# First projection units by feature block in a two-attention gated kernel on one Trainium2 core

## The chip, the core and the metric

The kernel runs on one core of one Trainium2 chip. The profile shows five engines and their queues: PE (matrix products; its weight loads are the row PEld), DVE (VectorE), ACT (ScalarE), POOL (GpSimd) and SP (SyncE), which here issues every DMA transfer. SBUF is the working memory, PSUM holds what PE writes, DRAM holds inputs, outputs and scratch. The metric is the device time of one execution in microseconds, lower is better; the time before is 1057.04 us, the median of three runs (1056.77 to 1057.28).

## The reference, cut to what matters

```python
x = A_x                                            # 1 x 2048 x 448
g = sigmoid((x * gate_w).sum(-1, keepdims=True))
# A: per-head feature maps (two softmaxes of q @ w_phi and k @ w_phi), then linear attention, @ wo
# B: softmax attention over all 2048 keys, 16 heads of 28
q, k, v = split_heads(x @ B_wqkv)
p = softmax(q @ k.T * 28 ** -0.5)
b = (p @ v).merged_heads @ B_wo
return g * a + (1 - g) * b
```

Everything is float32. The part that the change touches is `x @ B_wqkv` for the 896 columns of q and k of attention B.

## The kernel before

**Products in two parts.** A float32 operand is split into a high part of type fp32r and the rest. `XH` holds the high part of x (features on the partitions, in four blocks b of 128; positions along the free axis), `XL` the rest; a weight tile holds the high part in `w[:, 0]` and the rest in `w[:, 1]`. A product is high·high + low·high + high·low. The fourth block has only 64 features of its own: its upper 64 partitions hold a copy, from which the high part is taken away (L340), so that it needs two products. `x3` (L110) yields these in order, so a sum over 448 features takes 11 products (4 blocks × 3, less one).

**Projection units.** `UNITS` (L527) lists pairs (m, t): 128 columns of q and k, 512 positions. `proj_qk(n, ev)` (L532) takes a PSUM bank, runs the 11 products, copies the high part out on ACT (L540), takes the rest on DVE (L541), and stores both to DRAM (`qkd`, L542), from where later stages load heads. Units 0 to 3 are (m = 0..3, t = 0), units 4 to 7 are t = 1, units 8 to 11 t = 2, units 12 to 15 t = 3; then the columns m = 4.

**The start.** The raw data go through a pool `stg` of 4 buffers of [128, 2, 512]; the results of units through `ev`, 3 buffers. `load_cols(m)` loads 128 columns of the weight for all four feature blocks, `x_loads(t)` loads 512 positions of x in two transfers of two blocks. `splits(n)` splits the weight columns of unit n (n < 4) and x for t = n / 4 when n is a multiple of 4; it is called one unit ahead. The copies of high parts are on ACT, the subtractions on DVE, that of block 2 of x on GpSimd for t > 0 (L338). So unit 0 needs all of x's four blocks for t = 0 and the first 128 weight columns, unit 1 the next 128 columns, and so on.

**The loop** (L589) runs units 0 to 19. At n = 0, 4, 8 it asks for the next 512 positions of x; at n = 5 for `phi_s` and the four pieces of `wtk` (`load_fold`); at n = 10 for the second weight tile `wB1` and for the head tiles `qp`, `kp`, `kt` of the maxima; at n = 10, 12, 14, 17 it calls `fold`, which multiplies w_phi into a weight (L356) in a bank of the tag "s"; from n = 16 on `mx_unit` computes row maxima of q·k in tiles of two banks (`ps_mx`, two buffers).

**Who sets the order.** On PE, DVE, ACT and GpSimd instructions stand in the order of the program. On SP a planner sets the order of the transfers when the program is built; SP then works through that order, and a transfer whose condition isn't met holds up those behind it. Each transfer also waits until the one eight places before it in the queue has landed.

**PSUM banks.** `ps_s` (L61) hands out 3 banks by turns, `ps_pv` one bank, `ps_mx` two tiles of two banks each. A bank or tile can be written again when its readers are done.

**Later.** After the loop come the features of attention A, the folding of `wqA` (L717 to L721, in halves for the first two groups), the values, and from about 360 us on the scores of attention B.

Of the kernel before, what the change touches and what calls it, by code (L numbers as in the profile page):

```python
# [34 lines left out]
def f32(ap):  # L35
    return ap.bitcast(F32)
# [3 lines left out]
def gated_mix_kernel(ctx, tc, xT, wqkB, wvB, wvA, wkAT, wqAT, phi, woA, woB,  # L40
# [20 lines left out]
    def ps_s(nm):  # L61
        return ps.tile([P, 512], F32, tag="s", name=nm, bufs=psn[0])
# [266 lines left out]
    def split_x(t, raws):  # L329
        tt = slice(t * 512, (t + 1) * 512)  # L330
        for b, raw in zip((0, 2), raws):
            nc.scalar.copy(XH[:, b:b + 2, tt], raw)  # L332

            def low(b=b, raw=raw):
                if b == 0:
                    nc.vector.tensor_sub(XL[:, 0:2, tt], raw, f32(XH[:, 0:2, tt]))
                else:
                    (nc.gpsimd if t else nc.vector).tensor_sub(  # L338
                        XL[:, 2, tt], raw[:, 0, :], f32(XH[:, 2, tt]))
                    nc.vector.tensor_sub(XH[64:, 3, tt], raw[64:, 1, :], f32(XH[64:, 3, tt]))  # L340

            lows.append(low)
# [2 lines left out]

    def load_fold(src, nm):
        wts[nm] = bk.tile([112, NG, 512], F32, tag="wt", name=f"wt{nm}", bufs=1)
        for k in range(NG):
            nc.sync.dma_start(wts[nm][:, k, :], src[:, k, :])

# [181 lines left out]
    def proj_qk(n, ev):  # L532

        m, t = UNITS[n]
        tt = slice(t * 512, (t + 1) * 512)
        pq = ps_s(f"pqk{t}_{m}")
        w, c = wB[m // 4], m % 4 * P
        run(pq, [(w[:, i, b, c:c + P], x) for b, x, i in x3(tt)])
        e = ev.tile([P, 2, 512], F32R, tag="ev", name=f"ev{t}_{m}")
        nc.scalar.copy(e[:, 0, :], pq)  # L540
        nc.vector.tensor_sub(e[:, 1, :], pq, f32(e[:, 0, :]))  # L541
        nc.sync.dma_start(qk_d[m * P:(m + 1) * P, :, tt], f32(e))  # L542


    ev_s = ExitStack()
    ev = ev_s.enter_context(tc.tile_pool(name="ev", bufs=3))
    stg = ev_s.enter_context(tc.tile_pool(name="stg", bufs=4))
    wB[0] = weights(1, "wB0")
    wB[1] = ev.tile([P, 2, 4, 384], F32R, name="wB1", bufs=1)
    wkA_s = weights(2, "wkA_s")  # L550
    wvA_s = weights(3, "wvA_s")
    raws = {}

    def load_cols(m):
        raw = stg.tile([P, 2, 512], F32, tag="stg", name=f"wB0_raw{m}")[:, 0, :]
        raws[("c", m)] = raw = raw.rearrange("p (b n) -> p b n", n=P)
        nc.sync.dma_start(raw, wqkB[:, :, m * P:(m + 1) * P])

    def split_cols(m):
        split_weight(wB[0], raws.pop(("c", m)), slice(0, 4), slice(m * P, (m + 1) * P))  # L560

    def loads(key, *fns):
        raws[key] = [f() for f in fns]
# [9 lines left out]

    def splits(n):

        if n < 4:
            split_cols(n)
        if n % 4 == 0 and n < 16:
            split_x(n // 4, raws.pop(("x", n // 4)))
        if n in (13, 15):  # L580
            split_part(wB[1], "wB1", 384, (n - 13) // 2)
        take_lows()

    load_cols(0)
    x_loads(0)
    for m in (1, 2, 3):
        load_cols(m)
    splits(0)
    for n in range(NP):  # L589
        take_acts()  # L590
        if n in (0, 4, 8):
            x_loads(n // 4 + 1)
        if n == 5:
            nc.sync.dma_start(phi_s, phi)
            load_fold(wkAT, "k")
        if n == 10:
            part_loads("wB1", wqkB[:, :, 512:896], 384, "wB1")
        splits(n + 1)
        if n == 14:
            part_loads("wvA", wvA, 450, "wvA")  # L600
            nc.sync.dma_start(sel_s, sel)
            nc.sync.dma_start(mask_s, mask)
            for v in vap:
                nc.gpsimd.memset(v[:, :, 28:32], 0.0)
                nc.gpsimd.memset(v[:, :, 28:29], 1.0)
        if 16 <= n < 20:
            mx_unit()
        proj_qk(n, ev)
        if n in (16, 18):
            split_part(wvA_s, "wvA", 450, (n - 16) // 2)  # L610
            take_lows()
        if n == 0:
            pkv = ps_pv("pkv")
        if n in (10, 12, 14, 17):
            fold(wkA_s, "k", {10: 0, 12: 1, 14: 2, 17: 3}[n])
        if n == 10:
            pair_query(0, 0)
            pair_load(0, 0)
        if n == 15:
            pair_load(0, 1)  # L620
            pair_query(0, 1)
        if n in (14, 19):
            take_subs()
# [27 lines left out]
    for i in range(2 * NT + 11):  # L651
        t, q = i, i - NT
        y = q - 1
        tb = y // 2
        take_acts()
        if t < NT and t % 2 == 0:
            mx_unit()
            passes = (55 if t < NT - 4 else 44) + (4 if t >= 4 else 0)
            pace["n"], pace["at"] = 4 if t >= 4 else 0, [k * passes // 4 for k in (1, 2, 3)]
        if q in (0, 1):  # L660
            take_exps()

        if t % 2 == 0 and 0 <= t - 4 < NT:
            kv_add(t - 4)
            kv_add(t - 3)
        if q == 2:
            bk_s.close()
            ta_s = ExitStack()
            ta = ta_s.enter_context(tc.tile_pool(name="ta", bufs=1, reuse_waits="tile"))
            stg = ta_s.enter_context(tc.tile_pool(name="stg", bufs=2, reuse_waits="tile"))  # L670
            KV = ta.tile([112, 8, 64], F32, name="KV")
            kvT = kv_copy()
            ps_s_.close()
            ps = ps_s_.enter_context(tc.tile_pool(name="psq", bufs=1, space=PSUM, reuse_waits="tile"))
            psn[0] = 4
            woA_s = weights(3, "woA_s")
            wvB_s = weights(2, "wvB_s")
            take_exps()
        if t < NT:
            pk = ps_s(f"pk{t}")  # L680
            tok_major(pk, t, wkA_s, D, tick)
            fk[t] = features1(pk, f"k{t}", nc.gpsimd)
            take_exps(1)
        if 0 <= q < NT:
            pq = ps_s(f"pq{q}")
            tok_major(pq, q, wqA_s, D)
        if q == 0:
            fk[NT - 1] = features2(fk[NT - 1], f"k{NT - 1}")
        if q in (1, 2):
            fq[q - 1] = features2(fq[q - 1], f"q{q - 1}")  # L690
        if 0 <= q < NT:
            fq[q] = features1(pq, f"q{q}", nc.vector if 0 < q < 9 else nc.gpsimd)
        if 0 <= t - 1 < NT - 1:
            fk[t - 1] = features2(fk[t - 1], f"k{t - 1}")
        if q in (0, 1) or q >= 8:
            mx_unit()
        if y >= 9 and y % 2 and tb - 4 < 8:
            oTs[tb - 4] = normalize4(ta, num.pop(tb - 4), f"a{tb - 4}", 2)
        if q > 0:
            take_exps(int(q < NT))  # L700
        if q == 3:
            kv_out(kvT)
        if 2 <= q - 1 < NT:
            fq[q - 1] = features2(fq[q - 1], f"q{q - 1}")
        take_subs()
        if t == 1:
            pair_load(0, 3)
        if y >= 8 and y % 2 == 0 and tb - 4 < 8:
            num[tb - 4] = normalize3(*num[tb - 4], 2)
        if t < NT:  # L710
            value_a(t)
            if t % 2 and t < NT - 4:
                proj_qk(NP + t // 2, ev)
        if q in (0, 1):
            proj_qk(NP + 6 + q, ev)
        take_lows()
        if 2 <= i < 4:  # L717
            fold(wqA_s, "q", i - 2, 0, 2)
            fold(wqA_s, "q", i - 2, 2, 2)
        elif 4 <= i < 6:  # L720
            fold(wqA_s, "q", i - 2)  # L721
        if q == 1:
            ev_s.close()
        if q == 2:
            part_loads("woA", woA, D, "woA")
        if q == 11:
            part_loads("wvB", wvB, D, "wvB")
        if q in (4, 6):
            split_part(woA_s, "woA", D, (q - 4) // 2)
        if q in (14, 17):  # L730
            split_part(wvB_s, "wvB", D, (q - 14) // 3)
        if q == 1:
            gates()
        if y >= 4 and y % 2 == 0 and tb - 2 < 8:
            numer(tb - 2)
        if y < 9 or y % 2:
            if y >= 2 and y - 2 < NT:
                turn(y - 2)
        if 0 <= y - 10 < NT:
            out_a(y - 10)  # L740
            out_a2(y - 10)
        if y >= 9 and y % 2 == 0 and y - 2 < NT:
            turn(y - 2)
        if NT + 3 <= q < NT + 10:
            mx_unit()
        if q == NT + 2:
            bd_s.close()
            vb = [value_tile(0)]
        if 0 <= q - NT - 2 < 8:
            value_b(q - NT - 2)  # L750
        if y >= 5 and y % 2 and tb - 2 < 8:
            num[tb - 2] = normalize2(ta, *num[tb - 2], f"a{tb - 2}", 2, True)
# [383 lines left out]
```

## Time and profile before

| | |
|---|---|
| median of three runs | 1057.04 us |
| the profiled execution's own time | 1057.58 us |
| its span in the profile | 1055.8 us |
| PE busy | 1043.1 us |
| DVE, ACT, POOL busy | 705.1, 726.8, 227.7 us |
| moved by DMA | 99.03 MB |

The span runs from the first to the last instruction; what lies around it is 1.78 us here. Times in the rows are from the span's start. A row of the timeline has the start, the length, the engine, the line, what is written from what, how many instructions were merged (x2, x4), and in brackets how long the engine had stood idle and what released it. PE's products overlap, so that a product's rate is read from start to start, not from its length. In a row of windows stand, for each engine, the busy time and the number of instructions, then the granted TensorE clock, the share of the time in which the DMA engines moved packets, and the rate.

### The profile page before, as it was taken

The numbers are of one execution on the slowest core, as the hardware profiler recorded it, in microseconds if no ns is written. First come the engines' busy times: TensorE is split into PE (matmuls) and PEld (weight loads), VectorE is DVE, ScalarE is ACT, GpSimd is POOL, SyncE is SP. The second block draws the span as 40 slices with busy tenths as digits, with TensorE's granted clock in tenths as the row PEclk, the third lists the DMA queues.
The fourth block names the chain that finished last, engine by engine and source line by source line (L and its number), as shares of the span: only waits on it lengthen the run. The fifth ranks groups of instructions, "written<-read, shape, count | busy, mean of one in ns | idle before, by whom it ended". The sixth has DMA issues, their size and how long they took to land.

```text
span 1055.8 us, 16548 instructions
## 1 busy us (share of the span) xinstructions
PE 1043.1 (99%) x6328; PEld 566.3 (54%) x6328; DVE 705.1 (67%) x871; ACT 726.8 (69%) x879; POOL 227.7 (22%) x188
## 2 busy tenths in 40 slices
PE   7999999999999999999999999999999999999998
PEld 5878777878777643343343343343343343454545
DVE  4566776897855567777677677677677767777302
ACT  4455555577865777877777777777777777747572
POOL 0224544578635600120000000000000000000000
PEclk9999999999999999999999999999999999999999
DMA  8873010122232832233532324432233344132311
GB/s 274 282 254 107 30 50 29 41 64 89 81 111 92 188 70 53 56 77 79 118 66 72 73 60 145 111 69 71 62 69 80 80 108 106 46 115 62 95 63 53
DMA packets 65687, 99.03 MB, mean 94 GB/s; under 512 B 17976, under 2 KB 26792, under 8 KB 65608
## 3 DMA queue, kind: packets, MB, share of 16 engines
q1 hardware_dynamic: 65608, 97.97, 34.0%
q8 instruction: 50, 0.82, 0.3%
q14 instruction: 29, 0.24, 0.1%
HBM read 69.77 MB, written 27.78 MB: 92 GB/s over the span
## 4 chain that ended last, share of the span: by engine, by line
PE 93%; DVE 4%; POOL 1%; ACT 0%; DMA 0%; issue 0%; SPq 0%; DVEq 0%; ACTq 0%; POOLq 0%
PE st L804 27%; PE pv L907 24%; PE pm L306 10%; PE pqk L108 7%; PE poa L108 4%; PE pk L126 4%; PE pva L126 3%; PE pmb L267 3%; PE pob L108 3%; PE pvb L126 2%; PE pvb L108 2%; PE pq L108 1%; PE pn L505 1%; PE pft L493 1%; DVE featq L420 1%; DVE fsumq L429 1%
## 5 line engine op out<-in xcount | busy, mean ns | idle before, releaser
L806 ACT ACTIVATE p<-st 128x1024 f32<-128x1024 f32 x512 | 496.5, 1022 | 165.4 <-PE st L804 163.9
L314 DVE TENSOR_REDUCE part<-pm 128x3 f32<-128x1536 f32 (+1 forms) x241 | 421.9, 1751 | 169.0 <-PE pm L306 168.8
L804 PE MATMUL st<-qst,kst 128*128 128x512 f32 x1024 | 306.5, 421 | 0.0
L907 PE MATMUL pv<-p,vb 128*32 128x512 f32 x2048 | 272.7, 605 | 0.0
L804 PEld LDWEIGHTS st<-qst,kst 128*128 128x128 f32 x1024 | 172.4, 188 | 93.4 <-issue 67.8
L306 PEld LDWEIGHTS pm<-kc,qc 28*128 28x128 f32 x720 | 45.3, 181 | 199.5 <-DVE part L314 175.8
L272 DVE CUSTOM_DVE_ANT_0 rl<-pmb,rl 128x512 f32<-128x512 f32 x152 | 98.2, 684 | 54.7 <-ACT rl L270 54.5
L392 POOL TENSOR_TENSOR oUb<-oUb,rsb 128x512 f32<-128x512 f32 x15 | 19.3, 1287 | 517.6 <-DMA rsb<-rdb 220.5
L306 PE MATMUL pm<-kc,qc 28*128 28x512 f32 x720 | 121.3, 497 | 0.5 <-DVE part L314 0.5
L270 ACT ACTIVATE rl<-pmd 128x1024 f32<-128x1024 f32 x76 | 78.2, 1028 | 39.2 <-PE pmd L267 31.4
L907 PEld LDWEIGHTS pv<-p,vb 128*32 128x32 f32 x2048 | 40.3, 108 | 92.8 <-issue 92.1
L108 PE MATMUL pqk<-XH,wB 128*128 128x512 f32 x224 | 71.4, 409 | 6.7 <-ACT XH L332 6.7
L108 PEld LDWEIGHTS pqk<-XH,wB 128*128 128x128 f32 x224 | 42.3, 194 | 17.7 <-ACT XH L332 7.0
L540 ACT CAST ev<-pqk 128x512 fp32r<-128x512 f32 x28 | 16.4, 587 | 43.0 <-PE pqk L108 37.5
L108 PE MATMUL poa<-woA_s,oTa 128*128 128x448 f32 x192 | 43.4, 375 | 0.0
L126 PE MATMUL pk<-wkA_s,XH 128*128 128x448 f32 x128 | 39.4, 381 | 0.0
L541 DVE TENSOR_TENSOR ev<-pqk,ev 128x512 fp32r<-128x512 f32 x28 | 19.4, 691 | 29.6 <-ACT ev L540 29.5
L267 PE MATMUL pmd<-kp,qp 28*128 28x512 f32 x152 | 37.9, 494 | 0.7 <-DVE part L272 0.7
L108 PEld LDWEIGHTS poa<-woA_s,oTa 128*128 128x128 f32 x192 | 34.9, 188 | 6.3 <-issue 3.2
L267 PE MATMUL pmb<-kp,qp 28*128 28x512 f32 x152 | 38.0, 496 | 0.0
L126 PE MATMUL pva<-wvA_s,XH 128*128 128x450 f32 x128 | 37.8, 371 | 0.0
L108 PE MATMUL pq<-wqA_s,XH 128*128 128x448 f32 x128 | 37.4, 374 | 0.2 <-ACT oUa L368 0.2
(136 smaller groups left out, 1042.6 us busy)
## 6 DMA issues: line engine op xcount, KB each, us to landing
qkd<-ev SPq DMA_DIRECT2D x28, 512.0 KB
qst<-qkd SPq DMA_DIRECT2D x64, 224.0 KB
kst<-qkd SPq DMA_DIRECT2D x64, 224.0 KB
od<-oTb SPq DMA_DIRECT2D x48, 112.0 KB
xraw<-in_xT_dram SPq DMA_DIRECT2D x8, 512.0 KB
rsa<-rda SPq DMA_DIRECT2D x8, 512.0 KB
rsb<-rdb SPq DMA_DIRECT2D x15, 256.0 KB
gad<-ga SPq DMA_DIRECT2D x16, 224.0 KB
```

The source lines that it names most:

```text
L108: nc.tensor.matmul(dst, l, r, start=i == 0, stop=i == len(todo) - 1)
L126: nc.tensor.matmul(dst[:, :n], l, r, start=i == 0, stop=i == len(todo) - 1, skip_group_check=True)
L267: nc.tensor.matmul((pb if j < 2 else pd)[:, j % 2, :], qc[js, qt * P:(qt + 1) * P], kc[js, :], start=True, stop=True, tile_position=(32 * ...
L270: nc.scalar.activation(rl, pd, AF.Relu)
L272: nc.vector.tensor_tensor_reduce(rl[:, i, :], pb[:, i, :], rl[:, i, :], 1.0, LOWEST, ALU.add, ALU.max, part[:, col + i:col + i + 1])
L306: nc.tensor.matmul(pm[:, i, :], mxs[("qc", gq)][js, qt * P:(qt + 1) * P], mxs[("kc", g, kb)][js, :], start=True, stop=True, tile_position= ...
L314: nc.vector.tensor_reduce(part[:, col:col + n], pm[:, :n], AX.X, ALU.max)
L392: (nc.gpsimd if n == 1 else nc.vector).tensor_mul(oU, oU, rs)
L541: nc.vector.tensor_sub(e[:, 1, :], pq, f32(e[:, 0, :]))
L804: nc.tensor.matmul(st[:, jl, :], kst_of[(g, kt // 4)][:, j, (kt % 4) * P:(kt % 4 + 1) * P], qst_of[gq][:, j, :], start=True, stop=True)
L806: nc.scalar.activation(p, st, AF.Exp, scale=SCALE)
L907: nc.tensor.matmul(pv[32 * j:32 * j + 32, :], vb[kt // 8][:, kt % 8, 4 * g + j, :], pt[j // 2][:, j % 2, :], start=kt == 0, stop=kt == NT ...
```

## The change

Units 0 to 3 are computed together, by feature block. `first_units` loads, for each block b, 512 columns of the weight and 512 positions of x (256 KB each), and takes units 0 to 3 as four open sums in four banks: the three "s" banks and the "pv" bank. For block 0 the high part of x is made on DVE, that of the weight on ACT. For each block the 12 products (8 for the last) follow as soon as their operands are there. Ahead of them stand eight products of the identity with itself into the fourth bank, whose result is overwritten.

Units 4 to 6 write into banks of the two tiles of the maxima (`later`), which are not used before n = 16: units 4 and 6 in the two halves of one tile, unit 5 in the other.

x for t = 1 is split inside `first_units` (`splits(1)`), ahead of the evictions of units 0 to 3; x for t = 2 and t = 3 is split at n = 5 and n = 9, that is, one call ahead of units 4 and 8. Its loads are asked for at n = 4 and n = 6. The subtraction of block 2 is on DVE for t = 1 too.

Two copies of four numbers on GpSimd hold transfers back: one writes into `phi_s` from the first raw tile of x for t = 1, so that the load of `phi_s` waits until that tile is in; one writes from `phi_s` into `wtk`, so that the loads of `wtk` wait for `phi_s`.

`ev` has 4 buffers (one of them takes the raw data of the fourth block first), `stg` has 3. The first two groups of `wqA` are folded whole and no longer in halves.

```diff
-                    (nc.gpsimd if t else nc.vector).tensor_sub(
+                    (nc.gpsimd if t > 1 else nc.vector).tensor_sub(
                         XL[:, 2, tt], raw[:, 0, :], f32(XH[:, 2, tt]))
...
         wts[nm] = bk.tile([112, NG, 512], F32, tag="wt", name=f"wt{nm}", bufs=1)
+        if nm == "k":
+            nc.gpsimd.tensor_copy(wts[nm][:1, :, 0], phi_s[:1, :, 0])
...
-        pq = ps_s(f"pqk{t}_{m}")
+        pq = later.pop(0) if later else ps_s(f"pqk{t}_{m}")
         w, c = wB[m // 4], m % 4 * P
         run(pq, [(w[:, i, b, c:c + P], x) for b, x, i in x3(tt)])
+        keep_qk(m, t, pq, ev)
...
-    ev = ev_s.enter_context(tc.tile_pool(name="ev", bufs=3))
-    stg = ev_s.enter_context(tc.tile_pool(name="stg", bufs=4))
+    ev = ev_s.enter_context(tc.tile_pool(name="ev", bufs=4))
+    stg = ev_s.enter_context(tc.tile_pool(name="stg", bufs=3))
...
-        if n < 4:
-            split_cols(n)
-        if n % 4 == 0 and n < 16:
-            split_x(n // 4, raws.pop(("x", n // 4)))
+        if n % 4 == 1 and n < 12:
+            split_x(n // 4 + 1, raws.pop(("x", n // 4 + 1)))
...
+    def first_units():
+
+        raw = [stg.tile([P, 2, 512], F32, tag="stg", name=f"first_raw{b}") for b in range(3)]
+        raw.append(f32(ev.tile([P, 2, 512], F32R, tag="ev", name="first_raw3")))
+        for b in range(4):
+            nc.sync.dma_start(raw[b][:, 0, :], wqkB[:, b, :512])
+            nc.sync.dma_start(raw[b][:, 1, :], xT[:, b, :512])
+        x_loads(1)
+        pqs = [ps_s(f"pqk0_{m}") for m in range(3)] + [ps_pv("pqk0_3")]
+        pr = [ps_mx(f"pqk_{i}", False) for i in range(2)]
+        later.extend((pr[0][:, 0, :], pr[1][:, 0, :], pr[0][:, 1, :]))
+        for _ in range(8):
+            nc.tensor.matmul(pqs[3][:, :P], ident, ident, start=True, stop=True)
+        for b in range(4):
+            w, x = wB[0][:, :, b, :], XH[:, b, :512]
+            nc.scalar.copy(w[:, 0, :], raw[b][:, 0, :])
+            (nc.scalar.copy if b else nc.vector.tensor_copy)(x, raw[b][:, 1, :])
+            nc.vector.tensor_sub(w[:, 1, :], raw[b][:, 0, :], f32(w[:, 0, :]))
+            if b < 3:
+                nc.vector.tensor_sub(XL[:, b, :512], raw[b][:, 1, :], f32(x))
+                todo = [(0, x), (1, x), (0, XL[:, b, :512])]
+            else:
+                nc.vector.tensor_sub(x[64:], raw[b][64:, 1, :], f32(x[64:]))
+                todo = [(0, x), (1, x)]
+            if b < 3:
+                order = [(i, m) for i in range(3) for m in range(4)]
+            else:
+                order = [(i, m) for m in range(4) for i in range(2)]
+            for i, m in order:
+                nc.tensor.matmul(pqs[m], w[:, todo[i][0], m * P:(m + 1) * P], todo[i][1],
+                                 start=b == 0 and i == 0, stop=b == 3 and i == 1,
+                                 skip_group_check=True)
+        hold = raws[("x", 1)][0][:1, 0, :4]
+        splits(1)
+        nc.gpsimd.tensor_copy(phi_s[:1, :, 0], hold)
+        for m in range(4):
+            keep_qk(m, 0, pqs[m], ev)
+
+    later = []
+    first_units()
+    pkv = ps_pv("pkv")
+    for n in range(4, NP):
         take_acts()
-        if n in (0, 4, 8):
-            x_loads(n // 4 + 1)
+        if n in (4, 6):
+            x_loads(n // 2)
...
-        if 2 <= i < 4:
-            fold(wqA_s, "q", i - 2, 0, 2)
-            fold(wqA_s, "q", i - 2, 2, 2)
-        elif 4 <= i < 6:
+        if 2 <= i < 6:
             fold(wqA_s, "q", i - 2)
```

`keep_qk` holds the last four lines of the old `proj_qk` (copy, subtraction, store). In the order that the planner sets, SP issues the eight first loads, then the two tiles of x for t = 1 and the first of t = 2, then `phi_s`, the second tile of t = 2 and the first of t = 3, then the stores of units 0 to 4, the four loads of `wtk`, the store of unit 5, and the second tile of x for t = 3; from there the order is nearly that of before.

More of the change, by code (lines that the diff above doesn't have):

```diff
@@ L535, in proj_qk, with keep_qk @@
         tt = slice(t * 512, (t + 1) * 512)
-        pq = ps_s(f"pqk{t}_{m}")
+        pq = later.pop(0) if later else ps_s(f"pqk{t}_{m}")
         w, c = wB[m // 4], m % 4 * P
         run(pq, [(w[:, i, b, c:c + P], x) for b, x, i in x3(tt)])
+        keep_qk(m, t, pq, ev)
+    def keep_qk(m, t, pq, ev):
+        tt = slice(t * 512, (t + 1) * 512)
         e = ev.tile([P, 2, 512], F32R, tag="ev", name=f"ev{t}_{m}")
@@ L552, in gated_mix_kernel @@
     raws = {}
[L554 to L560, printed above, removed]
     def loads(key, *fns):
@@ L582, in splits @@
         take_lows()
[L584 to L589, printed above, removed]
+    def first_units():
[38 more added lines that the diff above has]
+    for n in range(4, NP):
         take_acts()
-        if n in (0, 4, 8):
-            x_loads(n // 4 + 1)
+        if n in (4, 6):
+            x_loads(n // 2)
         if n == 5:
@@ L611, in gated_mix_kernel @@
             take_lows()
-        if n == 0:
-            pkv = ps_pv("pkv")
         if n in (10, 12, 14, 17):
```

## The prediction

> **What bounds the kernel now.** I read the page first, then the chain of waits for the first 120 us, then the timelines of PE, ACT, DVE and SP up to 55 us, then windows over the same stretch.
>
> ```profile
> span 1055.8 us, 16548 instructions
> PE 1043.1 (99%) x6328; PEld 566.3 (54%) x6328; DVE 705.1 (67%) x871; ACT 726.8 (69%) x879; POOL 227.7 (22%) x188
> PE 93%; DVE 4%; POOL 1%; ACT 0%; DMA 0%; issue 0%; SPq 0%; DVEq 0%; ACTq 0%; POOLq 0%
> ```
>
> PE is the bound from beginning to end. So a microsecond that PE gains at the start is kept to the end, unless something with a clock of its own, the transfers, can't follow. The chain of the start:
>
> ```profile
> 0.74 0.68 SPq L557
> 1.48 4.06 DMA xraw<-in_xT_dram
> 5.56 1.05 ACT XH L332
> 6.66 1.22 PE pqk L108 x2
> 7.92 30.53 PE pqk L108 x119
> 38.45 0.88 PE pwk L356 x8
> ```
>
> PE stands for 6.66 us until x is in and split. Two things behind that hide in "PE busy". The first is the rate:
>
> ```profile
> 9.79 1.05 PE L108 MATMUL pqk<-XH,wB 128*128 128x512 f32 x2
> 10.64 0.63 PE L108 MATMUL pqk<-XL,wB 128*128 128x512 f32 x1
> ...
> 13.97 0.62 PE L108 MATMUL pqk<-XH,wB 128*128 128x512 f32 x2
> 14.44 0.40 PE L108 MATMUL pqk<-XL,wB 128*128 128x512 f32 x1
> ```
>
> From start to start two products take 0.85 us at 9.79 (0.425 each) and 0.47 us at 13.97. The evictions on ACT, one for each unit of 11 products, give the steady rate and the second thing, small stalls:
>
> ```profile
> 20.31 0.59 ACT L540 CAST ev<-pqk 128x512 fp32r<-128x512 f32 x1
> 23.15 0.59 ACT L540 CAST ev<-pqk 128x512 fp32r<-128x512 f32 x1 [2.25 <-PE pqk L108]
> 25.64 0.59 ACT L540 CAST ev<-pqk 128x512 fp32r<-128x512 f32 x1 [1.91 <-PE pqk L108]
> ...
> 30.63 0.59 ACT L540 CAST ev<-pqk 128x512 fp32r<-128x512 f32 x1
> 33.47 0.59 ACT L540 CAST ev<-pqk 128x512 fp32r<-128x512 f32 x1 [2.25 <-PE pqk L108]
> ...
> 41.91 0.59 ACT L540 CAST ev<-pqk 128x512 fp32r<-128x512 f32 x1
> 45.64 0.58 ACT L540 CAST ev<-pqk 128x512 fp32r<-128x512 f32 x1
> ```
>
> Unit 5 takes 25.64 − 23.15 = 2.49 us, 0.226 us a product. Units 4 and 8 (the first of a new t) take 2.84 us, 0.35 more, waiting for the split of x; unit 12 takes 3.73, less one fold (0.88) 2.85, 0.36 more. Unit 3 is evicted 0.2 us after its end, so unit 4 starts at 20.1. From 6.66 to 20.1 PE does 44 products in 13.4 us; at 0.226 they take 9.96. The other 3.5 us are the slow rate, which lasts until about 13.2, 6.5 us after the first product, and waits between.
>
> **The change part by part.**
>
> *Start and rate.* Eight products of the identity fill PE while it stands, from 1.3 on:
>
> ```profile
> 1.01 0.29 POOL masks.py:199 TENSOR_SCALAR_AFFINE_SELECT ident<-ident 128x128 f32<-128x128 f32 x1
> 4.14 0.62 ACT L142 CAST wB<-wB_raw 128x512 fp32r<-128x512 f32 x1 [2.13 <-DMA wB_raw<-in_wqkB_dram]
> 4.79 0.69 DVE L143 TENSOR_TENSOR wB<-wB_raw,wB 128x512 fp32r<-128x512 f32 x1 [3.90 <-ACT wB L142]
> L1000 PE MATMUL pd<-ident,rw 128*128 128x128 f32 x8 | 1.2, 288 | 0.0
> ```
>
> A float32 product of 128 columns is two records: 0.30 us by the last row (1.2 / 4), 0.22 by the fold (0.88 / 4, 112 columns). At the slow rate (0.425 / 0.226 = 1.88 times as long) eight take 3.3 to 4.5 us and end between 4.7 and 5.9. The first 256 KB were in at 4.14, the 512 KB behind them at 5.54, so 256 KB of x are in at about 4.85; the copy on DVE costs at most a DVE subtraction (0.69). The first real product then starts at 5.4 to 5.9; I take 5.5, against 6.66. Each block wants one more cast pair on ACT (2 × 0.62) and pair on DVE (2 × 0.69 = 1.4), less than its 12 products (2.7), so PE is not starved: DVE's nine instructions end by 11.6, while PE comes to the last block at 5.5 + 36 × 0.226 = 13.6.
>
> How long is the rate still low? Before, 6.5 us of PE work went by until it rose. Counted from 1.4 that is 7.9, a slow stretch of 2.4 us, which costs 2.4 × (1 − 0.226 / 0.425) = 1.1 us. At best it costs nothing. I take 0.6. Unit 4 then starts at 5.5 + 9.96 + 0.6 = 16.1 instead of 20.1: **−4.0 us** (−3.1 to −4.6).
>
> [...]
>
> *Old stalls.* x for t = 1, 2, 3 is split one unit or more ahead: **−1.06 us** (0.35 + 0.35 + 0.36).
>
> *Unit 6.* It shares a tile with unit 4, so it waits for unit 4's eviction on DVE. That stands behind the split of x for t = 2:
>
> ```profile
> 18.30 2.00 ACT L332 CAST XH<-xraw 128x1024 fp32r<-128x1024 f32 x2
> 19.39 1.22 DVE L336 TENSOR_TENSOR XL<-xraw,XH 128x1024 fp32r<-128x1024 f32 x1 [0.26 <-ACT XH L332]
> 20.64 1.68 DVE L340 TENSOR_TENSOR XH<-xraw,XH 64x512 fp32r<-64x512 f32 x1
> ```
>
> Units 0 to 3 end between 14.8 and 16.1; ACT evicts them until 17.35 and casts x until 19.35. DVE subtracts 1.22 until 19.6, then 1.68 (beside GpSimd) until 21.3, then evicts unit 4 until 22.0. PE wants unit 6 at 16.1 + 22 × 0.226 = 21.1: **+1.0 us**. Below: 0, if L340 takes a plain 0.69. Above: unit 4's eviction also needs the `ev` buffer of unit 0, stored at about 16.3. Stores behind a full queue are slow:
>
> ```profile
> 37.90 1.53 SPq L131 DMA_DIRECT2D wB_raw<-in_wqkB_dram  x2
> 44.91 0.83 ACT L142 CAST wB<-wB_raw 128x768 fp32r<-128x768 f32 x1 [2.41 <-DMA wB_raw<-in_wqkB_dram]
> ```
>
> 7.0 us from issue to use, against 3.4 for the first load (0.74 to 4.14). At 7.0 the store lands at 23.3 and PE waits until 24.6: 3.5.
>
> *First fold.* Its bank is freed by unit 8's eviction, which ACT and DVE reach after the split of x for t = 3. The second tile of that x is issued behind unit 5's store and four loads of `wtk`, at about 25.5, and lands 3.4 to 7.0 us later, at 28.9 to 32.5. Cast 1.0, subtraction 1.68, eviction 0.69: 32.3 to 35.9. PE wants the fold at 16.1 + 7 × 2.49 + 1.0 = 34.5, so 0 to 1.4: **+0.5 us**.
>
> *At nothing.* The two copies on GpSimd and the later `phi_s` and `wtk`: GpSimd has nothing else to do there, `wtk` goes out at some 22.6 and with 7.0 us is in at 29.6, before 34.5; without that cover each microsecond later costs one at the fold. What SP holds behind `phi_s` (until about 12) can't go earlier, since its buffers are free at 12 to 14. The whole folds of `wqA` keep their products on PE and save two casts and two subtractions that nobody waits for. The maxima from n = 16 on shift with PE if their loads do (a rival, below).
>
> Sum: −4.0 − 1.06 + 1.0 + 0.5 = **−3.6 us**. The profiled execution took 1057.58 (span 1055.8 and 1.78 around it), 0.54 above the median. It would go to 1054.0, the median 1057.04 to **1053.5**. Its own range, with the bounds above, is 1052 to 1055.
>
> **The rivals.** About 0.2%, 2.1 us, is what a measurement of this kernel can tell from no change.
>
> *The identity products don't count.* The rate then rises only 6.5 us after the first real product: slow from 5.5 to 12.0, which costs 3.1 instead of 0.6. Time: 1053.5 + 2.5 = 1056.0, no change. For it: before, PE worked from 6.66 to 9.8 with gaps and the rate stayed low, so light work may not do; against: eight float32 products in a row leave no gap. [...]
>
> *The transfers can't follow.*
>
> ```profile
> core 0: us, PE busy (x) PEld busy (x) DVE busy (x) ACT busy (x) POOL busy (x), PEclk, DMA share, GB/s
> 6.66:13.28 6.62, 6.58 (x15) 4.32 (x15) 3.67 (x5) 2.57 (x4) 0.00 (x0) 1.00 0.92 241
> 13.28:20.12 6.84, 6.84 (x32) 5.64 (x31) 3.62 (x6) 3.51 (x6) 0.00 (x0) 1.00 0.95 349
> 20.12:30.44 10.32, 10.32 (x46) 8.10 (x45) 5.68 (x7) 4.25 (x7) 1.39 (x1) 1.00 0.91 299
> 38.07:53.87 15.80, 15.80 (x81) 12.86 (x80) 9.89 (x12) 7.70 (x12) 5.30 (x11) 1.00 0.81 292
> ...
> 49.74 3.15 POOL L202 TENSOR_TENSOR kp<-kp,kt 28x512 fp32r<-28x512 f32 x2 [5.42 <-DMA kt<-qkd]
> 53.87 0.50 PE L267 MATMUL pmb<-kp,qp 28*128 28x512 f32 x2
> ```
>
> The DMA engines are busy for 81 to 95% of these windows. The first maximum unit comes 1.0 us after its operand is ready (49.74 + 3.15 = 52.89, used at 53.87). If that landing stays where it is, PE keeps 1.0 us: 1056.1, no change. Against it: in the last window a fifth of the time is free.
>
> *Slower: x for t = 3 lands too late.* One place, the first fold. From about 16 until that tile's landing the queue holds its 0.5 MB, another 0.5 of x, six stores (3.1) and `wtk` (0.9): 5.1 MB. At 299 to 349 GB/s they take 14.6 to 17.1 us and the tile lands at 31 to 33, as above. At 241 GB/s, the rate of the first window, they take 21.2, it lands at 37.2, and the fold stands until 40.6, 6.1 us: −4.06 + 6.1 = +2.0, 1059.0. It decides against the change below some 266 GB/s. For it: PE's earlier start, the stores of four units in a row. Against: the slow window is the one with weight columns in 512-byte pieces, which are gone.
>
> **How the numbers follow.** My forecast 0.64, identity products not counting 0.13, transfers 0.09, late x 0.14. Below 1054.9 lie nearly all of the first and a little of the second: faster 0.65; same is the rest of those, the third and a part of the fourth, 0.24; slower 0.11. The range runs from 1052.3, the better bounds together, to 1057.6, which takes in the two rivals of no change and the milder half of the late x.
>
> **What would show it.** Right: products 0.226 us apart by 8 us; unit 4's first product near 16; no wait for XL at units 4, 8, 12; waits of PE for DVE before units 6 and the first fold of about 1 and 0.5 us; the scores starting 3.6 us earlier than before. Wrong: 0.425 us between products beyond 9 us; ACT's cast of x for t = 3 waiting for its DMA beyond 33; the first maximum waiting for `kt`.

## The result, and the profile after

| | before | after |
|---|---|---|
| median of 22 runs each, side by side | 1056.68 us | 1054.74 us |
| ratio, 95% interval | | 0.9980 (0.9973 to 0.9987) |
| span of the profiled execution | 1055.8 us | 1053.2 us |

The change makes the kernel 1.94 us faster by the medians. That is a little less than the 2.1 us that the forecast took as the least that can be told from no change, but the interval of the ratio does not reach 1. A gain of 3.5 us was forecast, to 1053.5; the time is 1.2 us above that and inside the range.

The page of the changed kernel, its span, busy times and the shares of the chain of waits:

```profile
span 1053.2 us, 16588 instructions
...
PE 1042.9 (99%) x6344; PEld 568.8 (54%) x6344; DVE 705.6 (67%) x872; ACT 726.7 (69%) x878; POOL 227.3 (22%) x189
...
PE 93%; DVE 5%; ACT 1%; POOL 1%; DMA 0%; issue 0%; DVEq 0%; ACTq 0%; POOLq 0%
```

PE is as busy as before (1042.9 against 1043.1 us), in a span that is 2.6 us shorter: PE stood less at the start. The chain of waits up to 40 us (start, length, what) shows where, and what is new:

```profile
1.36 3.78 PE pqk L592 x16
5.14 9.53 PE pqk L609 x38
...
14.70 0.59 ACT ev L546
...
15.32 0.79 DVE ev L547 x2
16.10 5.14 DMA qkd<-ev
...
21.34 0.59 ACT ev L546
...
22.70 12.78 PE pqk L108 x55
35.49 1.21 issue
36.70 1.12 PE pwk L358 x8
```

PE has products from 1.36 on instead of 6.66. But the chain now leaves PE at 14.70 for a store: unit 0 is evicted, stored at 16.10, the store lands at 21.24, and only then does ACT evict unit 4, for which PE waits ahead of unit 6. PE's timeline of the changed kernel:

```profile
4.79 3.07 PE L609 MATMUL pqk<-XH,wB 128*128 128x512 f32 x8
7.70 1.07 PE L609 MATMUL pqk<-XL,wB 128*128 128x512 f32 x4
...
15.86 0.39 PE L108 MATMUL pqk<-XH,wB 128*128 128x512 f32 x1
...
22.70 0.73 PE L108 MATMUL pqk<-XH,wB 128*128 128x512 f32 x2 [1.70 <-DVE ev L547]
...
36.70 1.12 PE L358 MATMUL pwk<-phi_s,wtk 112*128 112x112 f32 x8 [1.21 <-issue]
...
52.08 0.50 PE L267 MATMUL pmb<-kp,qp 28*128 28x512 f32 x2
```

The first eight real products take 2.91 us (0.36 each), the next four 0.91 (0.227 each): the rate rises at about 7.1. Unit 4 starts at 15.86. Unit 6 would follow at 15.86 + 22 × 0.227 = 20.85 and starts at 22.70, 1.85 late; the fold would follow at 22.70 + 5 × 2.49 = 35.15 and starts at 36.70, 1.55 late. (The brackets have 1.70 and 1.21, since they count from the end of the last product.) ACT's, DVE's and SP's timelines of the same run say what was late:

```profile
21.34 0.58 ACT L546 CAST ev<-pqk 128x512 fp32r<-128x512 f32 x1 [2.70 <-DMA qkd<-ev]
...
34.10 1.05 ACT L332 CAST XH<-xraw 128x1024 fp32r<-128x1024 f32 x1 [4.48 <-DMA xraw<-in_xT_dram]
```

```profile
35.90 1.89 DVE L547 TENSOR_TENSOR ev<-pqk,ev 128x512 fp32r<-128x512 f32 x3
```

```profile
23.28 3.49 SPq L351 DMA_DIRECT2D wtk<-in_wkAT_dram  x4
...
27.43 0.61 SPq L131 DMA_DIRECT2D xraw<-in_xT_dram  x1
```

Ahead of the fold the view names no releaser ("issue"). DVE's row does: the first of its three evictions behind the late split of x for t = 3 runs from 35.90 to some 36.6, just ahead of the fold.

The first maximum unit comes at 52.08 against 53.87, 1.8 us earlier, and what is gained there stays to the end: the scores of attention B start at 359.7 us instead of 361.9.

### The profile page after: what moved, and what is told of

Read it like the earlier page. It is cut to its first block, busy times and chain, and to the rows that moved or that the text cites. A ratio compares the mean times of both kernels' runs of the same rounds, so it can differ in the third digit from the quotient of the medians.

```text
span 1053.2 us, 16588 instructions
## 1 busy us (share of the span) xinstructions
PE 1042.9 (99%) x6344; PEld 568.8 (54%) x6344; DVE 705.6 (67%) x872; ACT 726.7 (69%) x878; POOL 227.3 (22%) x189
## 4 chain that ended last, share of the span: by engine, by line
PE 93%; DVE 5%; ACT 1%; POOL 1%; DMA 0%; issue 0%; DVEq 0%; ACTq 0%; POOLq 0%
PE st L831 27%; PE pv L934 24%; PE pm L306 10%; PE pqk L108 5%; PE poa L108 4%; PE pk L126 4%; PE pva L126 3%; PE pob L108 3%; PE pmb L267 3%; PE pvb L126 2%; PE pvb L108 2%; PE pq L108 1%; PE pn L507 1%; PE pft L495 1%; PE pqk L609 1%; DVE rl L272 1%
## 5 line engine op out<-in xcount | busy, mean ns | idle before, releaser
L108 PE MATMUL pqk<-XH,wB 128*128 128x512 f32 x192 | 59.6, 397 | 1.7 <-DVE ev L547 1.7
L108 PEld LDWEIGHTS pqk<-XH,wB 128*128 128x128 f32 x192 | 35.3, 188 | 10.5 <-DVE ev L547 2.1
L948 DVE SCALAR_TENSOR_TENSOR acc<-pob,gate,acc 128x448 f32<-128x448 f32 x12 | 8.2, 684 | 41.6 <-PE pob L108 41.6
```

The source lines that it names most:

```text
L108: nc.tensor.matmul(dst, l, r, start=i == 0, stop=i == len(todo) - 1)
```

## The experiments

Each was run beside the kernel before on the same chip; ratios are to that kernel. A median is of 9 to 12 executions (5 for y1, 22 for the changed kernel). The positions are from PE's timeline of one profiled execution of each; "wait" is the idle time in the bracket of unit 6's first row, and "fell" says that the products behind a stand in the first 60 us were slow.

| run | unit 4 starts | wait ahead of unit 6 | first fold | first maximum | median, us | ratio (95%) |
|---|---|---|---|---|---|---|
| changed kernel | 15.86 | 1.70 | 36.70 | 52.08 | 1054.74 | 0.9980 (0.9973 to 0.9987) |
| x1 no identity | 17.06 | 0.44 | 36.14 | 51.53 | 1054.58 | 0.9983 (0.9974 to 0.9991) |
| x2 unit 6 in "s" | 15.33 | none | 35.77, fell | 52.78 | 1058.60 | 1.002 (1.001 to 1.003) |
| x3 stores of units 0 to 2 | 16.14 | 0.44 | 36.18 | 51.56 | 1053.79 | 0.9978 (0.9969 to 0.9987) |
| x4 x ahead of wtk | 15.06 | 2.06, fell | 36.48 | 51.79 | 1054.40 | 0.9979 (0.9970 to 0.9988) |
| x5 = x2 + x4 | 15.14 | none | 32.59, then 1.69, fell | 51.45 | 1056.85 | 1.0002 (0.9992 to 1.0012) |
| x6 = x4 + filler | 15.17 | 1.29 | 35.55 | 50.89 | 1056.40 | 0.9997 (0.9988 to 1.0005) |
| x7 = x2 + x3 + x4 | 15.66 | none | 33.12 | 49.19 | 1055.06 | 0.9979 (0.9969 to 0.9989) |
| x8 = x7, no identity | 17.07 | none | 34.52 | 50.88 | 1055.08 | 0.9987 (0.9978 to 0.9996) |
| y1 = x7, other bank | 15.21 | none | 32.67 | 49.05 | 1052.51 | 0.9964 (0.9952 to 0.9977) |
| y2 = y1, no identity | 16.20 | none | 33.65 | 49.80 | 1054.09 | 0.9976 (0.9967 to 0.9985) |
| y3 folds in halves | 15.12 | 2.55, fell | 36.83 | 52.15 | 1055.04 | 0.9983 (0.9974 to 0.9992) |
| y4 no holds | 16.10 | 3.97, fell | 40.65 | 55.97 | 1058.62 | 1.0022 (1.0012 to 1.0031) |

### x1: without the identity products

```diff
-        for _ in range(8):
-            nc.tensor.matmul(pqs[3][:, :P], ident, ident, start=True, stop=True)
```

> The eight identity products are left out (their result is overwritten in any case). Theory: the rate rises some 5.8 to 6.5 us after PE's first work of any kind, so without them it rises at 10.6 to 11.3 us instead of about 7.1; 14 to 15 products instead of 5.5 run at 0.425 us, unit 4's first product starts at 17.4 to 17.8 instead of 15.86 and the time is 1.6 to 1.9 us longer than the changed kernel's, since the store of unit 0 and with it the waits behind shift along. Rival 1, the identity products don't count: unit 4 starts at 15.9 and the time stays. Rival 2, the waits at unit 6 and the first fold take it up: unit 4 starts later but the first fold stands where it did (36.7), the time stays within 0.5 us.

```profile
4.82 3.75 PE L607 MATMUL pqk<-XH,wB 128*128 128x512 f32 x8 [4.82 <-DVE XH L594]
8.37 1.56 PE L607 MATMUL pqk<-XL,wB 128*128 128x512 f32 x4
...
17.06 0.62 PE L108 MATMUL pqk<-XH,wB 128*128 128x512 f32 x2
...
22.65 0.73 PE L108 MATMUL pqk<-XH,wB 128*128 128x512 f32 x2 [0.44 <-DVE ev L547]
```

In PE's timeline of this run the first eight products take 3.55 us (0.44 each), the next four 1.40 (8.37 to 9.77, 0.35 each), and the rate rises near 9.4, not at 10.6 to 11.3. Unit 4 starts 1.2 us later than in the changed kernel, but unit 6 at 22.65 against 22.70, and the time is the same: rival 2. The store of unit 0 did not shift along. It went out 1.1 us later and landed in time for ACT to evict unit 4 at 20.56 (21.34 in the changed kernel). So the identity products do bring the full rate forward, and in the changed kernel the wait for unit 0's store takes up what they bring.

### x2: unit 6 in a bank of its own

```diff
-        later.extend((pr[0][:, 0, :], pr[1][:, 0, :], pr[0][:, 1, :]))
+        later.extend((pr[0][:, 0, :], pr[1][:, 0, :]))
```

> Unit 6 goes into a bank of the tag s, so it shares no tile with unit 4. Unit 4's eviction still needs the buffer that unit 0's store gives back. Theory: PE's wait of 1.85 us ahead of unit 6 is gone (unit 6 starts at 20.9), but unit 4's eviction stays at 21.3, the store of unit 4 and what SP holds behind it stay, the second tile of x for t = 3 still lands near 34.1, and the first fold waits 3.2 instead of 1.4 us: the fold stays near 36.7 and the time within 0.4 us of the changed kernel's. Rival: the wait ahead of unit 6 is a loss of its own and the time falls by 1.5 to 1.9 us.

PE's timeline, then a row of windows:

```profile
35.77 1.41 PE L358 MATMUL pwk<-phi_s,wtk 112*128 112x112 f32 x8 [2.83 <-issue]
```

```profile
35.70:40.00 4.30, 4.23 (x16) 3.64 (x17) 1.79 (x3) 0.53 (x1) 1.20 (x9) 0.60 0.76 251
```

The wait ahead of unit 6 was gone and came back at the fold, as the theory had it. What no theory had: behind the stand of 2.83 us the granted clock was 0.60 for 4.3 us, and the first maximum came 0.7 us later than in the changed kernel. The time is longer by 0.4% than the changed kernel's rather than the same. Near 200 us PE stood once more, for the eviction of the last projection unit:

```profile
200.70 0.67 PE L108 MATMUL pq<-wqA_s,XH 128*128 128x448 f32 x2 [2.20 <-DVE ev L547]
201.21 0.37 PE L108 MATMUL pq<-wqA_s,XL 128*128 128x448 f32 x1
```

Here the products behind it kept their rate (0.5 us for the first two, then 0.2 each). The eleven executions spread from 1055.39 to 1060.31 us, and the mean granted clock goes with the time: 0.999 in the first, 0.998 in the four up to 1057.29 (the profiled one among them), 0.995 to 0.997 in the six above. So the other executions may have had more or longer falls than the profile shows.

### x3: buffers that do not wait for unit 0's store

```diff
-        e = ev.tile([P, 2, 512], F32R, tag="ev", name=f"ev{t}_{m}")
+        e = (ev.tile([P, 2, 512], F32R, tag="ev", name=f"ev{t}_{m}") if t or m > 2 else
+             wvA_s.rearrange("p i b n -> p (i b n)")[:, m * 1024:(m + 1) * 1024]
+             .rearrange("p (i n) -> p i n", n=512))
```

> The results of units 0 to 2 go through memory of a weight tile that is not yet in use, so the four buffers are free for units 3 to 6; unit 6 still shares a tile with unit 4. Theory (the buffer held by unit 0's store is what delays unit 4's eviction): ACT evicts unit 4 at about 18.7 instead of 21.3, DVE after the subtraction of x for t = 2 at 20.7, PE's wait ahead of unit 6 falls from 1.85 to about 0.6 us. All that SP holds behind unit 4's store is issued 1.2 us earlier, the second tile of x for t = 3 lands at about 32.9, the fold starts at 35.4 and the time falls by 1.0 to 1.3 us. Rival A, as forecast: the long subtraction beside GpSimd (1.68 us) delays that eviction, so the wait stays at 1.85. Rival B: that tile's landing is set by what the DMA engines have to move, it stays at 34.1, the fold at 36.7 and the time stays.

PE's timeline, then ACT's:

```profile
21.73 0.73 PE L108 MATMUL pqk<-XH,wB 128*128 128x512 f32 x2 [0.44 <-DVE ev L549]
...
36.18 1.12 PE L358 MATMUL pwk<-phi_s,wtk 112*128 112x112 f32 x8 [1.66 <-issue]
```

```profile
18.83 0.59 ACT L548 CAST ev<-pqk 128x512 fp32r<-128x512 f32 x1
...
33.58 1.05 ACT L332 CAST XH<-xraw 128x1024 fp32r<-128x1024 f32 x1 [4.93 <-DMA xraw<-in_xT_dram]
```

ACT evicts unit 4 at 18.83 and the wait falls from 1.70 to 0.44: the store of unit 0 was the cause, not the subtraction beside GpSimd (rival A), which accounts for no more than the 0.44 left. The fold gains 0.5, not 1.2, since the tile of x for t = 3 is in only 0.5 earlier (rival B in the main). The time (0.9978) is not told apart from the changed kernel's (0.9980); a fall of 1.0 to 1.3 us was expected.

### x4: x for t = 3 ahead of wtk

```diff
-        if n in (4, 6):
-            x_loads(n // 2)
+        if n in (4, 5):
+            x_loads(n - 2)
```

> Both tiles of x for t = 3 are asked for one unit earlier, which puts the second ahead of the four loads of wtk on SP; nothing else moves there but the store of unit 5, which comes behind wtk. Theory: it is issued at about 23.3 instead of 27.4, lands at 29 to 30, its split ends by 32, PE waits for nothing at the first fold (35.3 instead of 36.7) and the time falls by 1.2 to 1.4 us; the wait ahead of unit 6 stays at 1.85. Rival: wtk, now 0.6 us later, or the store of unit 5 lands later and takes the wait's place; the fold stays at 36.5 or beyond and the time stays.

Windows of this run, the stand and what follows, then PE's timeline:

```profile
19.80:22.20 2.40, 0.41 (x2) 0.00 (x0) 1.20 (x2) 0.59 (x1) 0.57 (x1) 1.00 1.05 403
22.20:26.00 3.80, 3.73 (x9) 2.98 (x10) 0.71 (x2) 0.59 (x1) 0.00 (x0) 0.55 1.02 357
```

```profile
22.27 1.22 PE L108 MATMUL pqk<-XH,wB 128*128 128x512 f32 x2 [2.06 <-DVE ev L547]
...
36.48 1.04 PE L358 MATMUL pwk<-phi_s,wtk 112*128 112x112 f32 x8
```

The wait at the fold is gone, and nothing is gained. PE came to unit 6 a little sooner, stood 2.06 us instead of 1.70, and the clock fell to 0.55: the products are 0.43 us apart until 26, which costs 3.8 × 0.45 = 1.7 us. Neither the theory nor its rival had this. Not every execution fell: five of the eleven had a mean granted clock of 1.000 and took 1053.21 to 1054.06 us, six had 0.998 and took 1054.40 to 1056.13. The first five are about 1 us below those executions of the changed kernel that kept 0.999 or more (median 1054.4), close to what the theory promised.

### x5 and x6: both edits together, and a filler in the wait

x5 has the edits of x2 and x4. x6 has that of x4 and this:

```diff
+        if n == 6:
+            fill = ps_s("fill")
+            for _ in range(6):
+                nc.tensor.matmul(fill[:, :P], ident, ident, start=True, stop=True)
```

> Both single edits together: unit 6 in a bank of the tag s, and x for t = 3 ahead of wtk. Theory (each edit alone left one stand of PE of over 2 us, after which the granted clock fell to 0.55 to 0.60 for some 3.5 us; without either stand the clock stays): PE runs units 4 to 10 without a break at 1.00, the first fold starts at 33.0 to 33.6 against 36.7 in the changed kernel, and the time is 2.2 to 3.3 us below the changed kernel's, 2.2 if the operand of the first maximum stays at 49.9. Rival (the transfers set the pace of this whole stretch, so PE only waits elsewhere): the fold starts at 35.5 or later and the time falls by less than 0.8 us.

> x for t = 3 ahead of wtk as in the run before, and six products of the identity with itself, into a bank nobody reads, stand ahead of unit 6 while it waits for unit 4's eviction. Theory (the stand of 2.06 us, not the late transfer, cost that run its gain, since the clock fell to 0.55 behind it): unit 6 still starts at about 22.3, but its products come 0.227 us apart instead of 0.425, the first fold starts at 34.7 to 34.9 instead of 36.5 and the time is 1.5 to 1.8 us below that of the run without these products. Rival (the products were slow for another reason, the operands or DMA traffic of 357 to 403 GB/s in those windows): they stay slow, the fold stays at 36.5, and the time stays.

x6 first, PE's timeline and the window behind the wait:

```profile
20.16 1.50 PE L541 MATMUL fill<-ident 128*128 128x128 f32 x12
22.95 0.73 PE L108 MATMUL pqk<-XH,wB 128*128 128x512 f32 x2 [1.29 <-DVE ev L551]
```

```profile
22.90:26.40 3.50, 3.45 (x15) 2.88 (x16) 0.70 (x2) 1.18 (x2) 0.00 (x0) 1.00 0.80 270
```

With six identity products in the wait the clock stays at 1.00, and the fold comes 12.6 us after unit 6's start instead of 14.2. So it was PE's standing idle that made the products of x4 slow. The transfers alone, 357 GB/s in x4's slow window, do not: where PE ran without a break the clock read 1.00 beside 345 GB/s in y1 (21 to 27 us) and beside 405 in x5 (32.0 to 33.6). The time did not follow: it was expected 1.5 to 1.8 us below that of x4 and is 2.0 us above. x5, PE's timeline and one window:

```profile
32.59 1.04 PE L358 MATMUL pwk<-phi_s,wtk 112*128 112x112 f32 x8
35.32 0.73 PE L108 MATMUL pqk<-XH,wB 128*128 128x512 f32 x2 [1.69 <-DVE ev L547]
...
199.38 0.68 PE L108 MATMUL pq<-wqA_s,XH 128*128 128x448 f32 x2 [2.21 <-DVE ev L547]
```

```profile
35.30:39.50 4.20, 4.18 (x11) 3.31 (x12) 1.22 (x2) 0.92 (x2) 0.00 (x0) 0.59 0.99 306
```

The fold starts at 32.59, 4.1 us earlier than in the changed kernel and a little earlier than the theory said. Then the same kind of wait, for a buffer that an earlier unit's store gives back, stands behind the fold (1.69 us), and the clock falls again. Both runs then lose at a place that no expectation named: near 199 us PE stands 2.2 us ahead of a query product of attention A, and behind it products come 0.37 us apart (x5 from 200.24 to 202.48, x6 from 199.75 to 202.75) instead of 0.20 (x2 from 201.42 to 202.63). From 200 to 210 us the clock reads 0.83 in both. Their times stayed within 0.03% of the kernel before.

### x7 and x8: all three edits, with and without identity products

> All three single edits: unit 6 in a bank of the tag s, x for t = 3 ahead of wtk, the results of units 0 to 2 through memory of a later weight tile. Theory: with unit 6 in its own bank nobody waits for unit 4's eviction on PE, so the buffers are worth nothing more: first fold and time within 0.4 us of the run with two edits. Rival: earlier stores bring the later loads and the first maximum forward by up to 1.5 us more.

> All three edits, and the eight identity products left out. Theory (the identity products bring unit 4 forward by 1.2 us, 15.86 against 17.06, which the wait for unit 0's store took up in the changed kernel): with no such wait the 1.2 us reach the first fold, and the time is 0.8 to 1.2 us longer than with all three edits and the identity products. Rival: the transfers bound the stretch all the same, fold and time stay within 0.3 us.

x7, PE's timeline and the window behind its last row:

```profile
49.19 0.50 PE L267 MATMUL pmb<-kp,qp 28*128 28x512 f32 x2
...
197.49 1.05 PE L108 MATMUL pq<-wqA_s,XH 128*128 128x448 f32 x2 [2.20 <-DVE ev L549]
```

```profile
197.40:201.00 3.60, 3.51 (x10) 3.12 (x11) 1.89 (x6) 0.00 (x0) 1.47 (x1) 0.53 0.37 146
```

The rival won at the first maximum, by more than it said and by a path that it did not name: the fold is 0.5 us later than in x5, but the wait behind it falls from 1.69 to 0.49 and the clock stays at 1.00 (33 to 40 us), so the first maximum comes 2.3 us earlier (49.19 against 51.45). x2 and x5 to x8 all hand out one bank of the tag "s" more than the changed kernel, so the query product at 197 us got the bank that the last projection unit had just filled. The stand and the fallen clock cost 2.2 + 3.6 × 0.47 = 3.9 us, and the 2.9 us gained by 49 are lost. In x8 the fold is 1.4 us and the first maximum 1.7 us later than in x7, though the medians are alike and the intervals of the ratios overlap; x8's profile is of the slowest of its twelve executions (1058.60 us). So of its theory the fold came true, and the time neither shows nor excludes the 0.8 to 1.2 us.

### y1 and y2: the banks' turn kept

```diff
-        pq = later.pop(0) if later else ps_s(f"pqk{t}_{m}")
+        pq = later.pop(0) if later else (ps_pv if n == 6 else ps_s)(f"pqk{t}_{m}")
...
-    pkv = ps_pv("pkv")
     for n in range(4, NP):
+        if n == 8:
+            pkv = ps_pv("pkv")
```

with `later` cut as in x2, and the edits of x3 and x4. y2 leaves the identity products out.

> The three edits again, but unit 6 in the bank of the tag pv instead of one of the tag s, so that the banks of the tag s go round as in the kernels before and after. Theory (unit 6 in a bank of the tag s shifted which bank the query products of attention A get at about 197 us; there PE then stood 2.2 us for the eviction of the last projection unit, and the granted clock fell behind it; that took back what the first 50 us had gained): the first fold starts at 33.0 to 33.5, the first maximum unit at 49.0 to 49.5, no stand of 2.2 us near 197, and the time is 2.4 to 2.9 us below the changed kernel's. Rival: that stand comes from PE being earlier, not from the bank; it is there again and the time is within 0.8 us of the changed kernel's.

> As the run before, without the eight identity products. Theory: they are worth what they bring at unit 4 (1.2 us) once no wait takes it up: first fold and first maximum 1.2 to 1.7 us later than in the run before, and the time longer by as much. Rival: the transfers bound the stretch, the time stays within 0.5 us.

y1, PE's timeline and the window that fell in x7:

```profile
32.67 1.04 PE L358 MATMUL pwk<-phi_s,wtk 112*128 112x112 f32 x8
...
49.05 0.50 PE L267 MATMUL pmb<-kp,qp 28*128 28x512 f32 x2
```

```profile
197.40:201.00 3.60, 3.60 (x25) 3.37 (x25) 3.41 (x7) 1.07 (x2) 1.61 (x1) 1.00 0.37 146
```

No stand at 197, the clock at 1.00, the first maximum 3.0 us earlier than in the changed kernel, and 1052.51 us: the fastest of all, 2.2 us below the changed kernel by medians (1.7 by the ratios) and 0.36% below the kernel before. That is a little less than the 2.4 to 2.9 expected. The two intervals just touch, but all five executions of y1 (at most 1052.87) lie below all 22 of the changed kernel (at least 1053.65). The bank was the cause of the stand, not PE's being early. y2 is 1.58 us longer. Of this 0.75 are there at the first maximum and 1.1 at 225 us (226.64 against 225.51 at the same product); the rest comes later and no experiment explains it. With little wait left to hide it, most of the identity products' gain reaches the end.

### y3: the folds in halves again; y4: no holds

y3 undoes the last part of the change's diff. y4 takes out the two copies on GpSimd:

```diff
-        if nm == "k":
-            nc.gpsimd.tensor_copy(wts[nm][:1, :, 0], phi_s[:1, :, 0])
...
-        hold = raws[("x", 1)][0][:1, 0, :4]
...
-        nc.gpsimd.tensor_copy(phi_s[:1, :, 0], hold)
```

> The changed kernel with the first two groups of wqA folded in halves again (two more banks of the tag s handed out). Theory: the query products at 197 us then get a bank whose reader is long done, so no stand of 2.2 us; the time stays within 0.6 us of the changed kernel's, as the forecast had it. Rival: the whole folds are there to keep the banks' turn, and any other turn costs a stand and a fall of the clock: 2 to 4 us longer.

> The changed kernel without the two copies on GpSimd that hold phi_s and wtk back; on SP phi_s and wtk then stand between the tiles of x for t = 2 and t = 3, ahead of all stores. Forecast: nothing. Theory now: the second tile of x for t = 3 is issued about 4 us earlier, the wait at the first fold (1.4 us) goes; the wait ahead of unit 6 stays at 1.7 to 2.1 us, and if it passes some 1.9 us the clock falls behind it and 1.75 us are lost: time between 1.4 below and 0.5 above the changed kernel's. Rival (what the holds are for): the early loads push x for t = 1 and 2 back, PE waits for XL at units 4 or 8, and the time is 0.5 to 2 us longer.

y3's time is not told apart from the changed kernel's, so the halves were worth nothing either way. Up to the first fold of wqA it is the changed kernel, and it shows how thin the margin there is. PE's timeline and a window of y3:

```profile
22.81 1.22 PE L108 MATMUL pqk<-XH,wB 128*128 128x512 f32 x2 [2.55 <-DVE ev L547]
...
36.83 1.04 PE L358 MATMUL pwk<-phi_s,wtk 112*128 112x112 f32 x8
```

```profile
22.80:26.40 3.60, 3.59 (x10) 2.88 (x11) 0.69 (x1) 0.51 (x1) 0.00 (x0) 0.58 0.91 294
```

The rate rose earlier this time (unit 4 at 15.12), PE stood 2.55 us at unit 6 and the clock fell; the fold starts where it did. Here too some executions kept the clock: three of eleven had a mean of 1.000 and took 1053.27 to 1053.73 us, eight had 0.998 and took 1054.55 to 1055.81. y4's chain of waits, then PE's timeline:

```profile
16.70 7.06 DMA qkd<-ev
...
25.22 15.59 PE pqk L108 x55
```

```profile
25.22 1.22 PE L108 MATMUL pqk<-XH,wB 128*128 128x512 f32 x2 [3.97 <-DVE ev L545]
...
40.65 1.04 PE L356 MATMUL pwk<-phi_s,wtk 112*128 112x112 f32 x8
```

Without the holds the kernel is slower than before the change. Units 4 and 8 wait for nothing, so it is not the rival's mechanism. The 1.1 MB of `phi_s` and `wtk` go ahead of unit 0's store, which takes 7.06 us instead of 5.14; PE stands 3.97 us and 55 products take 15.59 us instead of 12.78.

## Why the prediction came out as it did

**Start and rate: −4.0 forecast, −4.2 measured.** Right in the mechanism; that the number fits so closely is luck in part, since two errors cancel: real products start at 4.8 to 5.1, not 5.5, and the slow rate cost 5.5 products × 0.2 = 1.1 us, the top of its bound. Over ten runs with identity products unit 4 starts between 15.06 and 16.14, over three without between 16.20 and 17.07. By the same count as in the changed kernel the rate rises at about 5.4 to 7.7 us in the ten and at about 8.0 to 9.5 in the three (an estimate from start-to-start times: the first eight products take 2.11 us in x4 to 3.17 in x3, and 3.34 in y2 to 3.55 in x1). No run here shows what sets the moment within that spread.

**Old stalls: −1.06.** Right: 55 products of units 6 to 10 take 12.78 us in one piece, unit 8 among them, and no row waits for XL.

**Unit 6: +1.0 forecast, +1.85 measured.** This step failed in its cause. The forecast let the split of x for t = 2 delay unit 4's eviction, and had the buffer of unit 0 only as an upper bound (3.5, with the 7.0 us of a load; the store took 5.14). x3 shows that the buffer is the cause of all but 0.44 of the 1.70 us wait. That the store lands near 21 whether it goes out at 15.6, 16.1 or 17.2 us (ACT's eviction at 20.86, 21.34 and 20.56 in x2, the changed kernel and x1) fits that neither an earlier PE nor the identity products gain anything here. What sets that landing was not tested.

**First fold: +0.5 forecast, +1.55 measured.** The mechanism was right, the size was beyond the bound of 1.4. The second tile of x for t = 3 went out at 27.43 instead of 25.5: `wtk` could start only at 23.28 instead of 22.6, behind the late store of unit 4, and its four loads took SP 3.49 us. The tile was in 6.7 us after its issue, within the forecast's 3.4 to 7.0.

**At nothing.** The folds: right (y3). The holds: right that they cost nothing, but the step asked only what they cost; y4 shows that the changed kernel without them is 3.9 us longer by the medians. That was the slower case that the forecast lacked: a transfer ahead of a store whose buffer PE needs.

**The sum.** By the first fold −4.2 − 0.7 + 1.85 + 1.55 = −1.5 (measured 36.70 − 38.29 = −1.6), with unit 12's stall −1.9 by the first maximum (−1.8), and −1.94 by the medians. The two new waits are 1.9 us larger than forecast; that is the miss.

**The rivals.** "The identity products don't count": wrong as put, since the rate rises some 2.3 us later without them (x1, 9.4 against 7.1); yet in the changed kernel they are worth nothing at the end. "The transfers can't follow" at `kt`: no, in y1 the first maximum comes 3.0 us earlier still. "x for t = 3 too late" came true in a mild form, 1.55 instead of 6.1 us. Of the signs named as wrong, one is there: ACT's cast of x for t = 3 waits for its DMA until 34.10, beyond 33. Of the signs named as right, the scores start 2.2 us earlier, not 3.6.

**What the whole forecast lacked** is that a stand of PE can cost more than its length. Behind most stands of 1.7 to 2.8 us the products were slow: in x2, x4, x5, x7 and y3 windows of 3.6 to 4.3 us read 0.53 to 0.60 of the clock, some 1.5 to 1.7 us more. It is no part of the miss in the profiled execution, which stood 1.70 and escaped; y3, the same program there, did not. Among the 22 executions of the changed kernel six have a mean granted clock of 0.997 or 0.998, so some of them probably fell.

## What to carry to other kernels

When a change takes work off the front of a stretch, look for the next thing with its own clock, here a buffer that only a store's landing gives back; a gain that runs into it is gone, and single edits behind it can show nothing until the waits of the stretch are removed together (x2, x4 and x5 gained nothing in their medians, y1 gained 2.2 us by medians). Price a stand of PE of about 2 us with the slow products that may follow it (1.5 to 1.7 us in the windows here). And where buffers go round by turns, taking one more out of the ring changes the partners of every later user: x2 and x5 to x8 lost 2.2 to 3.9 us near 200 us to an edit at 20 us.

## What the runs showed of the hardware that was not expected

The granted clock can fall after short stands. It read 1.00 in the windows behind the stands of 0.49 us (x7), 1.29 (x6) and 1.70 (changed kernel), and products kept 0.23 us behind those of 0.44 (x1, x3) and 1.66 (x3) and 0.20 behind one of 2.20 (x2, at 200.70). The stands of 1.69 (x5), 2.06 (x4), 2.20 (x7), 2.55 (y3) and 2.83 (x2) were followed by windows of 3.6 to 4.3 us at 0.53 to 0.60. Behind those of 2.20 (x8) and 2.21 (x5, x6) near 199 us products came 0.37 us apart instead of 0.20, and behind that of 3.97 (y4) 0.43 us apart until 31.3, 6.1 us. So between 1.69 and 2.20 us it goes either way, also from one execution to the next (x4, y3, by mean clocks of 1.000 and 0.998), and no run here shows what decides. At the start the clock column does not help: it reads 1.00 from 6.66 to 13.28 us of the kernel before, where products came 0.425 us apart, and from 4.8 to 8.4 in x1, where they came 0.44 apart.

From its issue to the use of its buffer, unit 0's store of 512 KB took 3.3 us in x1 (17.24 to 20.56); its landing took 5.14 us in the changed kernel and 7.06 in y4, where 1.1 MB of loads more had been issued ahead of it. In the 2.4 us before unit 6's start in x4 the DMA engines moved 403 GB/s, with a share of the time that the view gives as 1.05.
